# Queries and keys in fp16 parts scaled by a power of two per batch, eight head pairs in plain float32, in an attention and MLP kernel

## The chip, the core and the metric

The kernel runs on one core of a Trainium2 chip. The metric is the device time of one execution in microseconds (us). The engines are TensorE (PE, matmuls; its weight loads are listed as PEld), VectorE (DVE), ScalarE (ACT), GpSimd (POOL) and SyncE (SP), whose queue issues the DMA transfers here, in order.

## The reference

A batch of 8 with 8 heads of 64 dimensions has 512 local and 32 global tokens. Global queries attend to all 544 keys, local queries to the 32 global keys and to local keys at most 32 positions away. The output rows then go through a two-layer MLP with Mish. Cut to what matters:

```python
k_all = np.concatenate([k_g, k_l], axis=2); v_all = np.concatenate([v_g, v_l], axis=2)
s_g = scale * np.matmul(q_g, k_all.transpose(0, 1, 3, 2))      # 32 x 544 per head
out_g = np.matmul(sm(s_g), v_all)
s_ll = np.where(mask, scale * np.matmul(q_l, k_l.transpose(0, 1, 3, 2)), -1e9)   # |i - j| <= 32
s_lg = scale * np.matmul(q_l, k_g.transpose(0, 1, 3, 2))
out_l = np.matmul(sm(np.concatenate([s_lg, s_ll], axis=-1)), v_all)
x = np.concatenate([out_g, out_l], axis=2)      # to 4352 rows of 512
h = x @ w_in                                    # 512 -> 2048
return (h * np.tanh(np.log1p(np.exp(h)))) @ w_out
```

## The kernel before, in words

Attention runs over 8 batches `b` of 4 head pairs `hp`, and each pair has 4 query tiles `t` of 128 rows. One (b, hp, t) is a unit; there are 128. For a unit, both heads' scores `s` (L608, in PSUM tiles of the ring `sc`) are formed on PE against a window of 192 (t = 0 and 3) or 224 (t = 1 and 2) keys. DVE adds the mask and takes the row maximum into `P` (L614), ACT takes the exponential (L623), ACT and DVE split the result into an fp16 part `ph` and a rest (L307, L642), a DMA transposes it into `pt`, and PE multiplies it with the values into `U` (L659). Once per pair the global queries' scores `g` (L697) are formed, normalised, transposed (`gpt`) and multiplied with the values (`gu`, L745). The normalised rows are split again and transposed by DMA into `xh` and `xl`.

The MLP runs over 17 blocks of 256 rows (two per batch, and one for the global rows), each in 8 steps. A step is 24 matmuls into `h` (L788: three products of the fp16 parts of weights and rows), Mish on ACT (`e`, L831), a split into fp16 parts `G` on DVE (L309, L844), and 12 matmuls into `o` (L856). One MLP step goes with one attention unit while there are any; the last steps stand alone at the end.

Float32 operands are multiplied as parts. Of a split pair, the keys come into `kraw` and the queries into `qraw`, each head's 64 dimensions twice, on 128 partitions. `ks` is a copy of the keys rounded to the type fp32r (L541, a cast at L300 on ACT or L302 on DVE), `kl` the rest (L546). `qs` holds the rounded query on the first 64 partitions and its rest on the others (L531, L538). A score is then two matmuls of 128 rows, `ks` with `qs` and `kl` with `qs`. `g_scores` takes four products for each stretch of keys, with `qgh`, the split global queries (L503). The first NPS = 5 pairs (all four of batch 0, and one of batch 1) are "plain": their queries and keys come once, in float32, and each head's score is one float32 matmul of 64 rows (L601).

At the start, the MLP weights come as 64-bit words and are put together into float32 in 32 blocks: DVE makes two of the three pieces (L384, L393), ACT converts the third into a buffer `wr` (L386), and GpSimd adds (L395). PE sums squares of the weights (L405) for a power-of-two scale, and then the weights are split into fp16 parts (L439 to L445). The first matrix must be ready before the first `h`, the second before the first `o`.

The order of all instructions on all engines, SP's queue too, is made ahead by a planner (class `Plan`). Each task is added with its engine or engines, an estimate of its time, and what it reads, writes and newly takes from a ring of buffers; a simulation then lets each engine start the task that can begin earliest, and of several the one that was added first. A few constants (`LATE_K`, `LATE_L`, `CONV2` and the like) shift groups of tasks. Tasks whose inputs and buffers are ready early are so drawn forward into idle time of the estimate. On the chip each engine then works strictly in that order.

## Time and profile before

| | |
|---|---|
| median of 3 runs | 1020.02 us (1020.01 to 1021.5) |
| profiled execution | 1018.93 us |
| its span, first to last instruction | 1017.1 us |
| PE busy | 925.7 us, 91% |
| DVE busy | 668.5 us, 66% |
| ACT busy | 680.9 us, 67% |
| GpSimd busy | 82.2 us, 8% |
| moved by DMA | 134.65 MB, mean 132 GB/s |
| mean granted clock of PE | 0.973 |

The profile is of one execution. A group's line gives line of code, engine, operation, output and inputs with shapes and count, then busy time in us and the mean ns of one, then the idle time of the engine before them and what ended it. Matmuls overlap one another, since a matmul's time includes that in which its last columns drain; the pace is read from their starts. A timeline row gives start and length in us, and merges several of a kind (x3).

### The profile page before, as it was taken

The numbers are of one execution on the slowest core, as the hardware profiler recorded it, in microseconds if no ns is written. First come the engines' busy times: TensorE is split into PE (matmuls) and PEld (weight loads), VectorE is DVE, ScalarE is ACT, GpSimd is POOL, SyncE is SP. The second block draws the span as 40 slices with busy tenths as digits, with TensorE's granted clock in tenths as the row PEclk, the third lists the DMA queues.
The fourth block names the chain that finished last, engine by engine and source line by source line (L and its number), as shares of the span: only waits on it lengthen the run. The fifth ranks groups of instructions, "written<-read, shape, count | busy, mean of one in ns | idle before, by whom it ended". The sixth has DMA issues, their size and how long they took to land.

```text
span 1017.1 us, 20581 instructions
## 1 busy us (share of the span) xinstructions
PE 925.7 (91%) x7906; PEld 664.6 (65%) x7906; DVE 668.5 (66%) x1704; ACT 680.9 (67%) x1321; POOL 82.2 (8%) x62
## 2 busy tenths in 40 slices
PE   3455696899999999999999999999999999999996
PEld 2233475566776777677777777777777777666663
DVE  6977796887766767776677666767676655322221
ACT  3465566777897788878878888788878888211110
POOL 3725231410000000000000000000000000000000
PEclk9997588999999999999999999999999999999999
DMA  9847982587758664766557665666676544100000
GB/s 333 228 111 175 262 259 63 112 180 189 168 104 180 144 143 113 177 148 143 123 153 161 134 133 129 155 135 141 117 165 127 123 81 77 42 1 22 1 22 21
DMA packets 231802, 134.65 MB, mean 132 GB/s; under 512 B 197528, under 2 KB 209048, under 8 KB 230680
## 3 DMA queue, kind: packets, MB, share of 16 engines
q1 hardware_dynamic: 231704, 133.34, 57.1%
q8 instruction: 62, 1.02, 0.4%
q14 instruction: 36, 0.29, 0.1%
HBM read 63.55 MB, written 8.91 MB: 71 GB/s over the span
## 4 chain that ended last, share of the span: by engine, by line
PE 65%; DVE 12%; DMA 8%; ACT 4%; issue 3%; SPq 1%; POOL 0%; ACTq 0%; DVEq 0%
PE o L856 28%; PE h L788 26%; PE s L608 4%; PE U L659 3%; DMA vraw<-in_vm 3%; DMA pt<-ph 2%; PE g L697 2%; DMA gpt<-gph 2%; PE gu L745 1%; DVE vmx L481 1%; DVE P L614 1%; DVE ph L642 1%; DVE G L309 1%; SPq L296 1%; DVE kl L546 1%
## 5 line engine op out<-in xcount | busy, mean ns | idle before, releaser
L856 PE MATMUL o<-W,G 128*128 128x512 f16 x1632 | 389.8, 379 | 0.3 <-POOL W L445 0.3
L788 PE MATMUL h<-xh,W 128*128 128x256 f16 x2048 | 379.0, 275 | 5.1 <-ACT e L831 5.1
L788 PEld LDWEIGHTS <-W 128*128 128x128 f16 x3264 | 311.2, 98 | 68.6 <-issue 5.3
L788 PE MATMUL h<-xl,W 128*128 128x256 f16 x1024 | 281.0, 274 | 0.0
L856 PEld LDWEIGHTS <-G 128*128 128x128 f16 x1632 | 156.9, 98 | 144.1 <-issue 0.6
L831 ACT ACTIVATE e<-h,c 128x512 f32<-128x512 f32 (+1 forms) x137 | 92.6, 683 | 117.5 <-PE h L788 116.6
L623 ACT ACTIVATE P<-P,nm 128x192 f32<-128x192 f32 (+1 forms) x256 | 117.8, 460 | 41.5 <-DVE nm L614 40.3
L309 DVE TENSOR_SCALAR G<-e,c 128x512 f16<-128x512 f32 x129 | 63.9, 495 | 118.5 <-ACT e L831 118.4
L614 DVE CUSTOM_DVE_ANT_0 P<-s,consts 128x192 f32<-128x192 f32 (+1 forms) x256 | 90.1, 367 | 68.1 <-PE s L608 57.7
L642 DVE SCALAR_TENSOR_TENSOR ph<-P,ph 128x384 f16<-128x384 f32 (+1 forms) x128 | 78.0, 611 | 80.1 <-ACT ph L307 79.3
L844 DVE SCALAR_TENSOR_TENSOR G<-e,c,G 128x512 f16<-128x512 f32 (+1 forms) x137 | 102.0, 745 | 3.4
L831 ACT ACT_TABLE_LOAD x79 | 101.4, 1283 | 1.4
L623 ACT ACT_TABLE_LOAD x74 | 94.9, 1283 | 1.3
L659 PEld LDWEIGHTS <-pt 96*128 96x128 f16 (+1 forms) x1536 | 59.3, 101 | 33.5 <-DMA pt<-ph 26.9
L307 ACT ACTIVATE ph<-P 128x384 f16<-128x384 f32 (+1 forms) x128 | 69.7, 548 | 16.3 <-DMA pt<-ph 13.2
L659 PE MATMUL U<-va,pt 128*128 128x64 f16 (+1 forms) x768 | 59.4, 199 | 19.7 <-DMA pt<-ph 19.7
L608 PE MATMUL s<-ks,qs 128*128 128x192 f32 (+1 forms) x216 | 71.4, 353 | 1.4 <-DVE qs L538 0.9
L659 PE MATMUL U<-vc,pt 96*128 96x64 f16 x768 | 58.7, 198 | 0.0
L718 ACT ACTIVATE gP<-g,gmx 64x288 f32<-64x288 f32 x64 | 30.4, 476 | 37.5 <-DVE gmx L713 37.4
L395 POOL TENSOR_TENSOR W<-W,wr 128x512 int32<-128x512 int32 x32 | 48.8, 1535 | 79.0 <-DVE W L393 40.1
L608 PE MATMUL s<-kl,qs 128*128 128x192 f32 (+1 forms) x216 | 54.2, 274 | 0.0
L405 PE MATMUL ws<-W 128*128 128x128 bf16 x128 | 17.7, 286 | 37.4 <-POOL W L395 37.3
(103 smaller groups left out, 1024.3 us busy)
## 6 DMA issues: line engine op xcount, KB each, us to landing
kraw<-in_kt SPq DMA_DIRECT2D x27, 640.0 KB, 4.7
qraw<-in_qt SPq DMA_DIRECT2D x27, 512.0 KB, 3.8
W<-in_w SPq DMA_DIRECT2D x19, 512.0 KB, 7.1
out<-ob SPq DMA_DIRECT2D x34, 256.0 KB, 2.6
vraw<-in_vm SPq DMA_DIRECT2D x8, 1024.0 KB, 6.0
wraw<-in_w SPq DMA_DIRECT2D x13, 512.0 KB, 5.9
vc<-vf SPq DMA_DIRECT2D x32, 128.0 KB, 2.3
va<-vf SPq DMA_DIRECT2D x32, 96.0 KB, 2.3
```

Source lines behind the costliest of these rows:

```text
L307: A.activation(out=dst, in_=src, func=AF.Copy, scale=c)
L309: V.tensor_scalar(dst, src, c, None, ALU.mult)
L395: pl.add(POOL, pool(512), lambda: G.tensor_tensor(f(), f(), X["wr", k], ALU.add), r=[("wr", k)], w=[key])
L608: T.matmul(X[s][:, :w], X[qs][:, h, t * 128:(t + 1) * 128], X[k][:, h, c0:c0 + w], start=(i == 0), stop=(i == 1))
L614: pl.add(DVE, 69 + 1.04 * w, lambda: V.tensor_tensor_reduce(out=X[P][:, h, :w], in0=X[s][:, :w], in1=mask[:, m0:m0 + w], scale=-SCALE, sca ...
L623: pl.add(ACT, 160 + 0.832 * w + 93, lambda: A.activation(out=X[P][:, h, :w], in_=X[P][:, h, :w], func=AF.Exp, bias=X[nm], scale=-1.0, accu ...
L642: pl.add(DVE, dve(n), lambda: V.scalar_tensor_tensor(p_part(X[ph], t, 1), p_src(X[P], t), PSC, p_part(X[ph], t, 0), ALU.mult, ALU.subtract ...
L659: T.matmul(X[u][:, t, h, :], X[pt][:k, p * 4 + h * 2 + c, :], X[vx][:k, t, vl, h * 64:(h + 1) * 64], start=(n == 0), stop=(n == 5))
L788: T.matmul(X[h][:, f * TB:(f + 1) * TB], wh(i, wl)[:, off:off + 128], X[x][:, d, o:o + TB], start=(n == 0), stop=(n == 11))
L831: chain(blk, i, ACT, 571, lambda a, z: A.activation(out=X[e][:, a:z], in_=hv(blk, i)[:, a:z], func=AF.Mish, bias=0.0, scale=X[c][:, 0:1]), ...
L844: chain(blk, i, DVE, 602, lambda a, z: V.scalar_tensor_tensor(gp(1, blk, i)[:, a:z], X[e][:, a:z], X["c", blk][:, 2:3], gp(0, blk, i)[:, a ...
L856: T.matmul(X[o], gp(g, blk, i)[:, f, t * 128:(t + 1) * 128], wh(8 + i, wl)[:, f * 512:(f + 1) * 512], start=(i == 0 and n == 0), stop=(i = ...
```

## The change

Queries and keys of the split pairs are now split into fp16 parts in place of fp32r. Since fp16 has a small range, keys are first multiplied by a power of two, and queries by its inverse, so that products stay as they are; one power per batch, chosen so that the largest query and the largest key of the batch get about the same size. It comes from a new input `mxs`, which holds all queries and keys of a batch once more in four tiles of 128 x 1088. `b_norm` loads these tiles, takes the largest absolute value of each on DVE, joins them across partitions on GpSimd and makes the two factors `sk` in some ten instructions on one column. It runs for batches 2 to 7. The first eight pairs, batches 0 and 1, are plain float32, in tiles `kn` and `qn` of their own, and need no factors; the four tiles of `mxs` go through the same buffers `kn` (`kraw` for batch 2). To make room, the ring `wr` goes from two buffers to one.

The estimate of the two score matmuls goes from `mm(2, 262)` to `mm(2, 235)`; all other estimates of steps that remain, and all constants, stand as they were.

```diff
-NPS = 5
+NPS = 8
...
-          ("wr", 2, [128, 512], I32),
+          ("wr", 1, [128, 512], I32),
...
-          ("qs", 2, [128, 2, SL], F32R), ("ks", 2, [128, 2, KW], F32R), ("kl", 2, [128, 2, KW], F32R),
-          ("qgh", 2, [128, 3, HP, 64], F32R), ("vgf", 2, [128, 2, 128], F16),
+          ("qs", 2, [128, 2, SL], F16), ("ks", 2, [128, 2, KW], F16), ("kl", 2, [128, 2, KW], F16), ("qgh", 2, [128, 2, HP, 64], F16),
+
+          ("qn", 2, [128, 2, SL], F32), ("kn", 2, [128, 2, KW], F32), ("mx4", 1, [128, 4], F32), ("m4", 1, [128, 4], F32),
+          ("sk", 2, [128, 4], F32), ("vgf", 2, [128, 2, 128], F16),
...
+    def b_norm(b):
+        mx, m, sk = ("mx4", b), ("m4", b), ("sk", b)
+        for i in range(4):
+            k = ("kn", "m", b, i)
+            ring = "kraw" if b == 2 else "kn"
+            pl.add(DMA, dma(544), lambda i=i, k=k: load(X[k].rearrange("p a n -> p (a n)")[:, :1088], mxs[b, i]), new=[(ring, k)])
+            pl.add(DVE, dve(1088), lambda i=i, k=k: V.tensor_reduce(
+                out=X[mx][:, i:i + 1], in_=X[k].rearrange("p a n -> p (a n)")[:, :1088], axis=AX.X, op=ALU.max,
+                apply_absolute_value=True), r=[k], w=[[mx, i]] if i else (), new=() if i else [("mx4", mx)])
...
     def q_hi(b, hp):
-        pl.add(COPY(1024, b), 0, lambda e: copy(e, X[qs], X[q]), r=[q], new=[("qs", qs)])
+        pl.add(COPY(1024, b), 0, lambda e: scaled(e, X[qs], X[q], X["sk", b][:, 0:1]), r=[q, ("sk", b)], new=[("qs", qs)])
...
     def k_lo(b, hp, h):
-        pl.add(DVE, dve(640), lambda: V.tensor_tensor(X[kl][:, h], X[k][:, h], X[ks][:, h].bitcast(F32), ALU.subtract),
-               r=[k, ks], w=[[kl, h]], new=() if h else [("kl", kl)])
+        pl.add(DVE, dve(640), lambda: V.scalar_tensor_tensor(X[kl][:, h], X[k][:, h], X["sk", b][:, 1:2], X[ks][:, h], ALU.mult, ALU.subtract),
+               r=[k, ks, ("sk", b)], w=[[kl, h]], new=() if h else [("kl", kl)])
...
-        pl.add(PE, mm(2, 262), go, r=[qs, ks, [kl, h]], new=[("sc", s)])
+        pl.add(PE, mm(2, 235), go, r=[qs, ks, [kl, h]], new=[("sc", s)])
...
-        if u == 11:
-            for n in range(HP, NPS):
-                plain_load(1, n - HP, "ks", kt0, KW)
-                plain_load(1, n - HP, "qs", qt0, SL)
+        if u in (8, 15):
+            for n in ((4, 5), (6, 7))[u == 15]:
+                plain_load(1, n - HP, "kn", kt0, KW)
+                plain_load(1, n - HP, "qn", qt0, SL)
...
+            if hp == (b > 1) and t == 2:
+                b_norm(b + 1)
```

`q_lo`, `k_hi` and `g_split` change in the same way, and `g_scores` uses the two fp16 parts that `qgh` now holds.

Three places show what moves. First PE, in batch 4, pair 2, tile 1: `gu` are the global values of the pair before, `s` the scores by batch, pair, tile and head. Before:

```order
L745 LDWEIGHTS vf_4_1_5765
L745 MATMUL gu_4_1_6435<-gpt_4_1_6400,vf_4_1_5765 128x64
L608 MATMUL s_4_2_1_0_6453<-ks_4_2_5949,qs_4_2_5895 128x224
L608 MATMUL s_4_2_1_0_6453<-kl_4_2_5960,qs_4_2_5895 128x224
L608 MATMUL s_4_2_1_1_6456<-ks_4_2_5949,qs_4_2_5895 128x224
L608 MATMUL s_4_2_1_1_6456<-kl_4_2_5960,qs_4_2_5895 128x224
L659 LDWEIGHTS pt_4_1_3_6339
```

In the changed kernel:

```order
L780 MATMUL gu_4_1_6532<-gpt_4_1_6486,vf_4_1_5816 128x64
L643 LDWEIGHTS qs_4_2_5946
L643 MATMUL s_4_2_1_0_6548<-ks_4_2_6000,qs_4_2_5946 128x224
L643 LDWEIGHTS qs_4_2_5946
L643 MATMUL s_4_2_1_0_6548<-kl_4_2_6011,qs_4_2_5946 128x224
L643 LDWEIGHTS qs_4_2_5946
L643 MATMUL s_4_2_1_1_6553<-ks_4_2_6000,qs_4_2_5946 128x224
```

The fp32r matmuls carry their weight load with them; the fp16 ones have a weight load as an instruction of its own ahead of each, like all other fp16 matmuls here.

Second, SP's queue in the start-up, just after the transposes `xh`, `xl` of batch 0's last pair, which the first `h` needs. `W` and `wraw` are weight blocks, `kn_m_2` the new tiles for batch 2. Before:

```order
L467 DMA_TRANSPOSE xl_0_638<-xs_0_3_1125 128x4x128
L296 DMA wraw_28_1167<-in_w2 128x1024
L296 DMA W_70<-in_w2 128x1024
L296 DMA qraw_1_1_1194<-in_qt 128x1024
L467 DMA_TRANSPOSE pt_1_0_1_1217<-ph1_73 128x8x128
L296 DMA kraw_1_2_1239<-in_kt 128x1280
L296 DMA wraw_30_1264<-in_w2 128x1024
L296 DMA W_70<-in_w2 128x1024
```

In the changed kernel:

```order
L469 DMA_TRANSPOSE xl_0_618<-xs_0_3_1113 128x4x128
L298 DMA W_70<-in_w2 128x1024 x2
L469 DMA_TRANSPOSE pt_1_0_1_1175<-ph1_73 128x8x128
L298 DMA kn_m_2_0_1200<-in_mxs 128x1088
L298 DMA W_70<-in_w2 128x1024
L298 DMA wraw_28_1232<-in_w2 128x1024
L298 DMA qraw_2_0_1263<-in_qt 128x1024
L298 DMA kn_m_2_1_1271<-in_mxs 128x1088
L469 DMA_TRANSPOSE gpt_1_0_1310<-gph0_80 128x10x64
L298 DMA W_70<-in_w2 128x1024
L298 DMA kn_m_2_2_1360<-in_mxs 128x1088
L298 DMA wraw_30_1395<-in_w2 128x1024
```

The loads of batch 1's split pairs are gone from this place; the tiles of `mxs` stand there in turn with the last weight blocks, three more of which now come after these transposes than before.

Third, DVE in batch 2, pair 1. `c` are the MLP's factors, `vf` the split values, `P` the row maximum of scores. Before:

```order
L770 TENSOR_TENSOR c_4_3023<-sv_2_2366,iw_67 128x1
L772 TENSOR_SCALAR c_4_3023<-sv_2_2366,sw_68 128x1
L642 SCALAR_TENSOR_TENSOR ph0_72<-P_2_1_0_2976,ph0_72 128x4x96
L561 SCALAR_TENSOR_TENSOR vf_2_2_3066<-vraw_2_2173,sv_2_2366,vf_2_2_3066 128x4x128
L614 ISA P_2_1_1_3089,nm_2_1_1_0_3090<-s_2_1_1_0_3070,consts_65 128x224
```

In the changed kernel:

```order
L805 TENSOR_TENSOR c_4_3110<-sv_2_2398,iw_67 128x1
L514 TENSOR_REDUCE mx4_4_3114<-kn_m_4_0_2956 128x1
L807 TENSOR_SCALAR c_4_3110<-sv_2_2398,sw_68 128x1
L514 TENSOR_REDUCE mx4_4_3114<-kn_m_4_1_2999 128x1
L649 ISA P_2_1_1_3160,nm_2_1_1_0_3161<-s_2_1_1_0_3138,consts_65 128x224
L649 ISA nm_2_1_1_0_3161 128x1
L596 SCALAR_TENSOR_TENSOR vf_2_2_3158<-vraw_2_2260,sv_2_2398,vf_2_2_3158 128x4x128
```

Reduces for batch 4 stand inside batch 2, two batches ahead of their use, between steps that feed the units. Of the 24 reduces, five stand before the first row maximum of batch 2, 14 between it and that of batch 3 (the rest of batch 3's, all of batches 4 and 5, and three of batch 6), and five after.

More of the change, by code (lines that the diff above doesn't have):

```diff
@@ new lines, in g_split @@
+    def g_split(b):
+        q, rq, sk = ("qgh", b), ("qgraw", b), ("sk", b)
+        pl.add([(ACT, act(512)), (DVE, dve2(512))], 0, lambda e: scaled(e, X[q], X[rq][:, 1:3], X[sk][:, 0:1]), r=[rq, sk], new=[("qgh", q)])
+        for a, h in ((0, HI), (1, LO)):
+            pl.add(DVE, dve(256), lambda a=a, h=h: V.scalar_tensor_tensor(X[q][h, a], X[rq][h, 1 + a], X[sk][h, 0:1], X[q][h, a], ALU.mult,
+                                                                          ALU.subtract), r=[rq, sk], w=[[q, a]])
@@ L994, in slot @@
             b_scale(b + 1)
-            g_split(b + 1)
             b_split(b + 1)
```

61 lines of the change are left out of this document (40 added, 21 removed).

## The prediction

> **What bounds the kernel now.** I read the sums of the engines first, then the busy times by stage, then the timeline of TensorE to get the pace of each kind of matmul.
>
> ```profile
> PE 925.7 (91%) x7906; PEld 664.6 (65%) x7906; DVE 668.5 (66%) x1704; ACT 680.9 (67%) x1321; POOL 82.2 (8%) x62
> ```
>
> The windows, in the columns PE, PEld, DVE, ACT, POOL, granted clock, DMA share and GB/s, say where that share is limiting.
>
> ```profile
> 120.00:132.00 12.00, 7.44 (x50) 4.98 (x47) 10.82 (x22) 6.56 (x17) 5.87 (x4) 0.50 1.03 266
> ...
> 140.00:160.00 20.00, 16.10 (x154) 14.14 (x152) 18.73 (x35) 11.38 (x21) 5.12 (x3) 1.00 0.57 172
> 160.00:180.00 20.00, 14.61 (x124) 10.87 (x123) 11.97 (x31) 14.41 (x20) 3.48 (x4) 0.83 0.36 75
> 180.00:200.00 20.00, 17.31 (x153) 11.30 (x152) 17.85 (x31) 13.83 (x30) 10.81 (x5) 1.00 0.46 83
> 200.00:220.00 20.00, 17.77 (x146) 11.03 (x145) 15.91 (x44) 15.43 (x35) 4.38 (x3) 1.00 0.89 189
> 220.00:320.00 100.00, 97.93 (x917) 72.16 (x916) 73.35 (x201) 77.75 (x153) 0.91 (x2) 1.00 0.71 154
> 320.00:840.00 520.00, 516.23 (x4685) 381.21 (x4683) 367.02 (x1002) 426.65 (x809) 1.40 (x4) 1.00 0.64 139
> ...
> 880.00:1017.00 137.00, 127.16 (x868) 84.74 (x866) 31.35 (x56) 21.57 (x32) 0.00 (x0) 0.98 0.05 16
> ```
>
> From 220 us on PE idles 2.1 us of 100 and then 3.8 us of 520, at full clock. What shortens PE's own work there comes off the end, so long as the others keep up; DVE is at 73% and 71%, ACT at 78% and 82%. From 140 to 220 us PE lacks 3.9, 5.4, 2.7 and 2.2 us (14.2 in all), with DVE as busy as 18.73 of 20: that is the end of the start-up, where other engines set the pace. The last stretch is MLP alone, which the change leaves.
>
> **The pace of the matmuls.** A matmul's own duration includes its drain, so I take starts. Two long runs from the chain of waits give the fp16 pace:
>
> ```profile
> 880.84 2.62 PE h L788 x24
> ...
> 1000.69 6.49 PE o L856 x30
> ```
>
> That is 109 ns for 256 columns and 216 ns for 512: 0.418 ns per column, hence 82 ns at 192 columns and 96 ns at 224. Now a fp32r score group (four matmuls: two heads, ks and kl), after `gu` and after `o`, on the timeline:
>
> ```profile
> 538.37 0.35 PE L608 MATMUL s<-ks,qs 128*128 128x224 f32 x1
> 538.56 0.27 PE L608 MATMUL s<-kl,qs 128*128 128x224 f32 x1
> ...
> 538.90 1.47 PE L856 MATMUL o<-W,G 128*128 128x512 f16 x6
> 540.01 0.45 PE L608 MATMUL s<-ks,qs 128*128 128x224 f32 x1
> ...
> 540.64 0.28 PE L788 MATMUL h<-xh,W 128*128 128x256 f16 x1
> ```
>
> After `gu` the group holds PE 538.90 - 538.37 = 0.53 us. After `o`, its first matmul begins while `o` drains, so I count both: 540.64 - 538.90 = 1.74 us, less six `o` at 0.216, leaves 0.44 us. The global scores `g`, with three fp16 U matmuls as a yardstick in the first two rows:
>
> ```profile
> 521.91 0.25 PE L659 MATMUL U<-va,pt 128*128 128x64 f16 x3
> 522.00 0.25 PE L659 MATMUL U<-vc,pt 96*128 96x64 f16 x3
> 522.09 0.43 PE L697 MATMUL g<-ks,qgh 128*64 128x256 f32 x2
> ...
> 522.59 0.24 PE L697 MATMUL g<-ks,qgh 128*64 128x32 f32 x2
> ...
> 522.79 0.42 PE L697 MATMUL g<-ks,qgh 128*64 128x256 f32 x2
> ...
> 523.30 0.28 PE L788 MATMUL h<-xh,W 128*128 128x256 f16 x1
> ```
>
> Twelve `g` matmuls take 1.21 us, the four short ones among them 0.20, 50 ns each, while three fp16 ones of 64 columns take 0.09 us, 30 ns each, although each brings its own 128-column weights. The weight loads differ, too:
>
> ```profile
> L608 PEld LDWEIGHTS s<-kl,qs 128*128 128x128 f32 x216 | 41.3, 191 | 2.2
> ...
> L659 PEld LDWEIGHTS <-pt 96*128 96x128 f16 (+1 forms) x1536 | 59.3, 101 | 33.5 <-DMA pt<-ph 26.9 <-issue 2.7
> ```
>
> So the fp32r group is held at about 110 ns per matmul whatever its width, and fp16 loads of 101 ns overlap down to 30 ns. The Trainium skill, "TensorE: Matmul & The Clock Gate", section "Weight-path perf modes — Fast Weight Load (FWL) and DoubleRow", puts the fast load on for 128 weight columns of any type but FP32; the 191 and 101 ns agree with that.
>
> **The change, part by part.**
>
> *Scores of the 24 pairs that stay split.* In fp16 a group costs 4 x 96 = 0.383 us at t = 1 and 2, 4 x 82 = 0.33 at t = 0 and 3. In each pair one group (t = 1) follows `gu`: 24 x (0.53 - 0.383) = 3.5 us. The other 72 average 0.347: 72 x (0.44 - 0.347) = 6.7 us. Sum -10.2 us.
>
> *Global scores.* Eight of 0.109 and four at the 30 ns pace are 0.99 us, so 24 x (1.21 - 0.99) = -5.3 us. The weights here have 64 columns, not 128; if the four short ones kept their 50 ns, 24 x 0.08 us of it would be lost, so the bounds are -3.4 and -5.3.
>
> *Three more pairs in plain float32.* The trace has these at the low clock:
>
> ```profile
> 126.93 3.96 PE L601 MATMUL s<-ks,qs 64*128 64x224 f32 x12
> 130.82 1.27 PE L697 MATMUL g<-ks,qgraw 128*64 128x256 f32 x4
> ```
>
> Twelve start within 3.89 us at clock 0.50 (window 120:132): 0.65 us a group of two, 0.33 at full clock, against 0.44 to 0.53. Twelve groups save 12 x 0.13 = 1.5 us; the `g` of these pairs I count even. They lie in 140 to 220 us, where PE has gaps: between 0 and -1.5, I take -1.5.
>
> *DVE.* Removed with three pairs, and added with each reduce and each scale:
>
> ```profile
> L844 DVE SCALAR_TENSOR_TENSOR G<-e,c,G 128x512 f16<-128x512 f32 (+1 forms) x137 | 102.0, 745 | 3.4
> ...
> L642 DVE SCALAR_TENSOR_TENSOR ph<-P,ph 128x384 f16<-128x384 f32 (+1 forms) x128 | 78.0, 611 | 80.1 <-ACT ph L307 79.3
> ...
> L546 DVE TENSOR_TENSOR kl<-kraw,ks 128x640 fp32r<-128x640 f32 x54 | 44.3, 821 | 0.2 <-ACT ks L300 0.2
> ...
> L538 DVE TENSOR_TENSOR qs<-qraw,qs 64x1024 fp32r<-64x1024 f32 x27 | 33.0, 1223 | 0.8
> ...
> L481 DVE TENSOR_REDUCE vmx<-vraw 128x1 f32<-128x512 f32 x32 | 20.6, 678 | 11.6 <-DMA vraw<-in_vm 11.6
> ...
> L485 DVE TENSOR_REDUCE vmx<-vgraw 128x1 f32<-128x128 f32 x8 | 2.2, 271 | 0.0
> ...
> L500 DVE TENSOR_TENSOR pmax<-pmax,p 128x1 f32<-128x1 f32 x8 | 1.2, 150 | 0.0
> ```
>
> Gone: 3 x (2 x 0.821 + 1.223) = 8.6 us besides the copies. The copies that remain become scaled copies of the same width, on the same two engines; I cost that at nothing. The subtraction becomes a three-operand instruction: the first two rows give (745 - 611)/128 = 1.05 ns a column, so 0.88 us for 640 columns instead of 0.82; about 0.06 us on each of three instructions in 24 pairs is 4 us over the whole run. New: a reduce over 1088 columns is 0.678 + 576 x 1.06 = 1.29 us ((678 - 271)/384 = 1.06 ns a column); four, and some ten small instructions of 0.15 us, for each of six batches: 40 us. The MLP and attention on PE hide them as long as DVE is not full. The order says where they stand: 5 of the 24 reduces before batch 2, 14 with three scale chains inside batch 2, 5 after. In batch 2 (220 to 320 us) DVE goes from 73.35 to 73.35 + 14 x 1.29 + 3 x 1.5 = 96 us, in a stage that PE, with 16 score groups and 4 global ones shortened, would finish in 97.4. Two stretches bound what that costs:
>
> ```profile
> 220.00:240.00 20.00, 20.00 (x196) 15.08 (x195) 18.48 (x61) 14.17 (x35) 0.56 (x1) 1.00 0.80 172
> ```
>
> Here DVE is at 92% and PE loses nothing; at 140:160 DVE is at 94% and PE loses 3.9 of 20, which over 100 us is 19. I take +3, near the first, which is the steady order; bounds 0 and 19. What waits behind a late reduce on DVE is the row maximum of the next scores, which frees the score banks that PE's next scores need.
>
> *Loads.* Each of the 24 new loads stands on SP's queue ahead of transposes and weight loads. With 43% of DMA time free at 160:220 on average and 36% at 320:840, I cost the steady ones at nothing; that cover is gone where DMA runs at 1.03, as at 120:132.
>
> *One `wr` buffer.* ScalarE may convert the next weight block only after GpSimd has added the last:
>
> ```profile
> 22.42 11.93 POOL L395 TENSOR_TENSOR W<-W,wr 128x512 int32<-128x512 int32 x8 [8.21 <-DVE W L393]
> 36.07 1.31 POOL L395 TENSOR_TENSOR W<-W,wr 128x512 int32<-128x512 int32 x1 [1.72 <-DVE W L393]
> 38.08 1.31 POOL L395 TENSOR_TENSOR W<-W,wr 128x512 int32<-128x512 int32 x1 [0.69 <-DVE W L393]
> ...
> L386 ACT ACTIVATE wr<-W x19: 654/679/701, 26.8 to 143.6; 128x512 int32<-128x512 uint32 x19
> ```
>
> Eight adds back to back take 1.49 us each, the next ones come every 2.01 us. An add of 1.31 and a conversion of 0.68 in turn, with two handovers, make about 2.2: 8 x 0.7 + 8 x 0.2 = 7 us later for the first matrix. It is needed only by the first `h`, which the last transposes of batch 0 hold until 132 us, so I take 0; bounds 0 and +7. Against it, the freed splitting can close up to about 9 of the 14.2 us that PE lacks there: -9.
>
> *Sum*, against the profiled execution (1018.93 us, its span 1017.1): -10.2 - 5.3 - 1.5 + 3 = -14.0, so 1004.9. The median of the three runs before, 1020.02, is 1.1 above the profiled one: forecast 1006.
>
> **The rivals.**
>
> *A: DVE overflows in batch 2, and the kernel is slower.* The new reduces are in order on DVE, so each also waits when its load is late. The nearest row:
>
> ```profile
> DVE vmx L481 <- DMA vraw<-in_vm: 11.6, 6, 3.3
> ```
>
> It shows 1.9 us a wait (the third number is the longest). With 14 x 1.9 = 27 us of waits beside 96 of work, DVE needs 25 us more than the 97.4 there are, and the kernel takes 1006 - 3 + 25 = 1028. It ends slower than before when a reduce waits over (17 + 1.4)/14 = 1.3 us on average. For it: the loads of several batches are drawn into batch 2. Against: only 6 of 32 reduces of `vmx` waited so, and a planned order that runs late on PE gives loads more time. Chance 0.16.
>
> *B: the start-up shortens as well.* 8.6 us and copies leave DVE where it is 94% busy; with 9 of the 14.2 us back the time is 997. Against: batch 2's first two pairs and five reduces move forward into the same place. Chance 0.16.
>
> *C: the start-up lengthens.* The single buffer's 7 us reach the first `h`, since DVE, ACT and SP work strictly in order: 1013. Chance 0.13.
>
> *D: fp16 weight loads do not overlap here*, so that the change does not do for the scores what it says. At the 101 ns of the load's row a group is 0.404 us and saves 72 x 0.036 + 24 x 0.126 = 5.6 instead of 10.2: 1011. Against: the U matmuls at 30 ns. Chance 0.05. The Trainium skill, "TensorE: Matmul & The Clock Gate", section "LDWEIGHTS (loading the stationary operand)", prices a load at its columns over 1.2 per ns, which is 107 ns for 128: by that rule as the pace the saving would be 3.3 us; the measured 30 ns pace speaks against reading it so.
>
> **How the numbers follow.** The forecast has 0.50, A 0.16, B 0.16, C 0.13, D 0.05. The forecast's own bounds are about 1000 to 1013. The range 995 to 1021 takes in B, C and D and the beginnings of A; what it leaves out is most of A (0.13) and the tail of B (0.04). A measurement of this kernel can tell about 0.2%, 2 us, from no change. Faster: 0.48 of the forecast, all of B and D, 0.10 of C: 0.79. Same: 0.02 of the forecast, 0.02 of C and 0.02 of A: 0.06. Slower: the rest of A and a rest of C: 0.15.
>
> **What would show it.** Right: score matmuls in fp16 at 82 and 96 ns from start to start, a `g` group near 1.0 us, PE still without gaps from about 220 us, DVE near 96 of 100 in batch 2, and the first `h` at 132 us, give or take 5. Wrong: a pace of 101 ns (D); gaps of PE in front of `s` in batch 2, ended by DVE, with reduces that wait for their loads (A); a first `h` several us later, behind ACT conversions that wait for GpSimd (C), or no gaps left before 220 us (B).

## The result, and the profile after

| | before | changed |
|---|---|---|
| median, same chip | 1020.76 us (1020.01 to 1023.34, 4 runs) | 1032.82 us (1030.22 to 1035.34, 4 runs) |
| ratio, 95% interval | | 1.0115 (1.0088 to 1.0142) |
| profiled execution, span | 1018.93, 1017.1 us | 1033.34, 1031.5 us |
| mean granted clock of PE | 0.973 | 0.952 |

Slower by 12 us, where the forecast was 14 less and its range ended at 1021. The sums of the engines on the page of the changed kernel:

```profile
PE 924.3 (90%) x7888; PEld 640.8 (62%) x7888; DVE 691.8 (67%) x1763; ACT 668.6 (65%) x1314; POOL 86.1 (8%) x68
```

A matmul's busy time includes its drain, so this sum hides what became of PE; the pace shows it. First a score group, second a group of `g` between two `h`, on the timeline of the changed kernel:

```profile
562.87 0.25 PE L643 MATMUL s<-ks,qs 128*128 128x192 f16 x1
...
563.20 0.25 PE L694 MATMUL U<-va,pt 128*128 128x64 f16 x3
...
564.76 0.27 PE L823 MATMUL h<-xh,W 128*128 128x256 f16 x1
564.96 0.41 PE L732 MATMUL g<-ks,qgh 128*64 128x256 f16 x2
...
565.42 0.21 PE L732 MATMUL g<-ks,qgh 128*64 128x32 f16 x2
565.48 0.21 PE L732 MATMUL g<-kl,qgh 128*64 128x32 f16 x2
...
565.77 0.38 PE L732 MATMUL g<-kl,qgh 128*64 128x256 f16 x2
566.08 0.28 PE L823 MATMUL h<-xh,W 128*128 128x256 f16 x1
```

The score group takes 563.20 - 562.87 = 0.33 us, as forecast. The `g` group takes 566.08 - (564.76 + 0.109) = 1.21 us, what it took in fp32r. Its short matmuls did come down to the 30 ns of `U` (0.06 us a pair); what was won is lost at its two ends: 564.96 is 0.09 us after the last `h` has gone through, and 566.08 comes 0.09 us after the last `g` (565.77 + 2 x 0.109).

The plain scores at full clock, in batch 1, on the timeline, and their row among the groups of the whole run:

```profile
220.60 0.65 PE L636 MATMUL s<-kn,qn 64*128 64x224 f32 x4
221.18 0.26 PE L694 MATMUL U<-va,pt 128*128 128x64 f16 x3
...
221.64 0.74 PE L636 MATMUL s<-kn,qn 64*128 64x224 f32 x4
222.31 0.39 PE L891 MATMUL o<-W,G 128*128 128x512 f16 x1
```

```profile
L636 PE MATMUL s<-kn,qn 64*128 64x192 f32 (+1 forms) x128 | 41.1, 540 | 12.8 <-DVE nm L649 8.3 <-DMA qn<-in_qt 4.4
```

Eight pairs of four tiles and two heads are 64 matmuls in the program; the trace lists 128. A float32 matmul leaves two records, so a group of four records is one tile: 0.58 and 0.67 us, more than the 0.44 to 0.53 of fp32r.

The windows that answer to those of before (PE, PEld, DVE, ACT, POOL, granted clock, DMA share, GB/s):

```profile
140.00:160.00 20.00, 17.40 (x147) 14.31 (x146) 19.37 (x28) 11.14 (x18) 8.96 (x6) 0.88 0.75 253
160.00:180.00 20.00, 14.23 (x134) 12.50 (x132) 13.28 (x37) 8.63 (x14) 4.07 (x5) 0.89 0.22 68
180.00:200.00 20.00, 16.97 (x136) 10.46 (x134) 16.78 (x30) 19.07 (x24) 6.91 (x4) 0.77 0.58 153
200.00:220.00 20.00, 18.22 (x126) 9.20 (x121) 13.93 (x31) 12.65 (x30) 10.97 (x5) 1.00 0.90 166
220.00:320.00 100.00, 93.00 (x827) 60.98 (x828) 76.79 (x214) 66.04 (x147) 2.18 (x3) 1.00 0.80 186
320.00:840.00 520.00, 510.00 (x4715) 364.34 (x4716) 391.08 (x1050) 420.00 (x808) 4.16 (x8) 1.00 0.69 151
```

PE now lacks 7.0 us at 220:320 (2.1 before) and 10.0 at 320:840 (3.8 before). From 140 to 220 it lacks 13.2, about as before, and the clock is down for longer: 0.88, 0.89 and 0.77 take 2.4 + 2.2 + 4.6 = 9.2 us of clock away (part of it while PE waits anyway), against 3.4 in the one window at 0.83. DVE, which I had at 96 of 100 at 220:320, is at 76.79. What PE waits for longest from 300 to 880 us, first in the changed kernel, then before (us in all, times, longest):

```profile
PE gu L780 <- DMA gpt<-gph: 6.2, 8, 1.4
PE U L694 <- DMA pt<-ph: 4.1, 6, 1.5
```

```profile
PE U L659 <- DMA pt<-ph: 3.9, 5, 1.8
PE gu L745 <- DMA gpt<-gph: 1.3, 4, 0.4
```

These are waits for transposed tiles: 10.3 us in place of 5.2.

The account below is made in the same way for every run of this case. For each profiled execution it has the start of the first `h`; PE's idle time from there to its last matmul; what half clock cost in between, which is half of PE's busy time in the stretches whose granted clock is 0.50; and the rest, PE's work from the first `h` on at full clock. The last matmul ends 10.0 to 10.5 us ahead of the end of the span in every kernel, and with these 10 us the four add up to the span.

| kernel | median us | ratio to before | span | first h | PE idle | half clock | PE work |
|---|---|---|---|---|---|---|---|
| before | 1020.8 | 1 | 1017.1 | 132.0 | 20.1 | 4.4 | 850.7 |
| changed | 1032.8 | 1.0115 | 1031.5 | 138.0 | 30.2 | 7.8 | 845.3 |
| after_wr2 | 1027.3 | 1.0053 | 1020.8 | 132.9 | 27.8 | 3.4 | 846.7 |
| before_wr1 | 1032.4 | 1.0112 | 1033.3 | 147.3 | 20.8 | 5.5 | 849.8 |
| after_no_norm | 1027.2 | 1.0054 | 1023.7 | 138.4 | 25.2 | 5.1 | 845.0 |
| after_no_norm_wr2 | 1019.2 | 0.9980 | 1020.5 | 134.6 | 23.7 | 6.9 | 845.1 |
| before_nps8 | 1030.9 | 1.0094 | 1028.2 | 133.1 | 23.3 | 6.0 | 855.8 |
| fp16_only | 1020.7 | 0.9996 | 1020.5 | 132.0 | 28.0 | 11.3 | 839.2 |
| after_g128 | 1032.6 | 1.0120 | 1033.8 | 138.9 | 34.5 | 11.4 | 839.0 |
| after_held | 1020.7 | 1.0002 | 1020.7 | 139.0 | 20.0 | 8.0 | 843.6 |
| after_wr2_held | 1012.4 | 0.9929 | 1007.8 | 133.5 | 16.3 | 2.7 | 845.2 |
| after_wr2_held_g128 | 1009.1 | 0.9891 | 1006.6 | 134.2 | 20.0 | 3.3 | 839.0 |
| fp16_only_late | 1010.8 | 0.9903 | 1009.0 | 144.7 | 14.4 | 4.3 | 835.2 |
| before_late | 1017.5 | 0.9969 | 1016.2 | 144.2 | 11.0 | 2.6 | 848.3 |
| after_late | 1030.3 | 1.0085 | 1028.3 | 147.9 | 17.0 | 10.1 | 843.4 |
| after_wr2_held_g128_late | 1034.8 | 1.0135 | 1036.3 | 139.8 | 37.9 | 10.7 | 838.0 |
| after_late_b3 | 1025.2 | 1.0044 | 1022.7 | 137.6 | 23.8 | 8.3 | 843.0 |
| after_wr2_held_g128_late_b3 | 1014.8 | 0.9946 | 1016.8 | 133.9 | 24.8 | 8.2 | 839.9 |

For the changed kernel: first `h` +6.0, idle +10.1, half clock +3.4, work -5.4, in all 14.1 of the 14.4 us between the two spans. Kernels that do the same matmuls agree within 4 us in the last column (843.0 to 846.7 for those with the changed kernel's matmuls); work before the first `h` is not in it, and the planner can move work across that point. A profiled span can also stand some us off its median: single runs of one kernel spread over 2 to 8 us.

### The profile page after: what moved, and what is told of

Its sections match the earlier page's. It is cut to its first block, busy times and chain, and to the rows that moved or that the text cites. A ratio compares the mean times of both kernels' runs of the same rounds, so it can differ in the third digit from the quotient of the medians.

```text
span 1031.5 us, 20592 instructions
## 1 busy us (share of the span) xinstructions
PE 924.3 (90%) x7888; PEld 640.8 (62%) x7888; DVE 691.8 (67%) x1763; ACT 668.6 (65%) x1314; POOL 86.1 (8%) x68
## 4 chain that ended last, share of the span: by engine, by line
PE 56%; DVE 14%; DMA 12%; ACT 5%; issue 3%; SPq 1%; POOL 0%; DVEq 0%; ACTq 0%
PE h L823 24%; PE o L891 23%; DMA gpt<-gph 5%; DMA pt<-ph 4%; PE U L694 2%; PE s L643 2%; PE g L732 2%; DMA vraw<-in_vm 2%; DMA kn_m<-in_mxs 1%; DVE ph L677 1%; DVE G L879 1%; PE gu L780 1%; DVE P L649 1%; DVE kl L581 1%; DVE mx L514 1%
## 5 line engine op out<-in xcount | busy, mean ns | idle before, releaser
L311 DVE TENSOR_SCALAR G<-e,c 128x512 f16<-128x512 f32 (+1 forms) x128 | 62.9, 492 | 117.9 <-ACT e L866 117.6
L694 PEld LDWEIGHTS <-pt 96*128 96x128 f16 (+1 forms) x1536 | 64.3, 102 | 40.9 <-DMA pt<-ph 30.0
L309 ACT ACTIVATE ph<-P 128x384 f16<-128x384 f32 (+1 forms) x128 | 69.5, 546 | 16.8 <-DMA pt<-ph 14.1
L397 POOL TENSOR_TENSOR W<-W,wr 128x512 int32<-128x512 int32 x32 | 46.6, 1457 | 78.3 <-ACT wr L388 28.6
L636 PE MATMUL s<-kn,qn 64*128 64x192 f32 (+1 forms) x128 | 41.1, 540 | 12.8 <-DVE nm L649 8.3
L658 ACT ACTIVATION_READ_ACCUMULATOR P<-P,nm 128x1 f32 x256 | 47.8, 187 | 0.0
```

Source lines behind the costliest of these rows:

```text
L309: A.activation(out=dst, in_=src, func=AF.Copy, scale=c)
L311: V.tensor_scalar(dst, src, c, None, ALU.mult)
L397: pl.add(POOL, pool(512), lambda: G.tensor_tensor(f(), f(), X["wr", k], ALU.add), r=[("wr", k)], w=[key])
L636: pl.add(PE, mm(1, 4 * w), lambda: T.matmul(X[s][:, :w], X[q][r, part, t * 128:(t + 1) * 128], X[k][r, part, c0:c0 + w], start=True, stop= ...
L658: pl.add(ACT, 160 + 0.832 * w + 93, lambda: A.activation(out=X[P][:, h, :w], in_=X[P][:, h, :w], func=AF.Exp, bias=X[nm], scale=-1.0, accu ...
L694: T.matmul(X[u][:, t, h, :], X[pt][:k, p * 4 + h * 2 + c, :], X[vx][:k, t, vl, h * 64:(h + 1) * 64], start=(n == 0), stop=(n == 5))
```

## The experiments

### The single buffer: after_wr2 and before_wr1

```
-          ("wr", 1, [128, 512], I32),
+          ("wr", 2, [128, 512], I32),
```

in the changed kernel; the reverse in the kernel before.

> The changed kernel with two wr buffers in place of one, and nothing else. Theory 1 (the single buffer delays the first weight matrix by 9 us, and that delay of the start-up stays to the end): GpSimd's adds come at 1.5 to 2.0 us again in place of 2.1, the sums of squares of the first matrix end near 52 us in place of 61.5, the first h falls back from 138 to about 132 us, and the median goes from 1032.8 to about 1022 to 1026. Rival (the loads and reduces of the largest values cause the loss, the buffer only fills time that was free): under 3 us, so 1030 to 1033.

> The kernel before with one wr buffer in place of two, and nothing else. Theory 1: the first matrix is ready about 9 us later, the first h comes 4 to 9 us later than 132 us, and the median is 1025 to 1030 against 1020.8. Rival (the buffer costs nothing, since the first h is held by batch 0's last transposes at 132 us): 1019 to 1023.

Measured: after_wr2 1027.29 us, 1.0053 (1.0038 to 1.0068); before_wr1 1032.38 us, 1.0112 (1.0091 to 1.0132). The first gains 5.5 us, a little less than the theory had, the second loses 11.5, more than it had. With one buffer the adds of the changed kernel come at a fixed pace (timeline of GpSimd):

```profile
37.63 1.33 POOL L397 TENSOR_TENSOR W<-W,wr 128x512 int32<-128x512 int32 x1 [0.79 <-ACT wr L388]
39.76 1.33 POOL L397 TENSOR_TENSOR W<-W,wr 128x512 int32<-128x512 int32 x1 [0.80 <-ACT wr L388]
```

That is 2.13 us an add, the 2.2 of the prediction. What it does to PE is seen in the longest wait of before_wr1 between 100 and 150 us:

```profile
PE ws L405 <- POOL W L395: 16.6, 7, 4.8
```

The sums of squares wait 16.6 us (4.7 before), and the first `h` starts at 147.3, 15 us late. In the changed kernel the same buffer costs 5.1 us of first `h`. So the 7 us of delay do reach the first `h`; that batch 0's transposes would cover them is refuted, and the size depends on the order around them: 5 in one, 15 in the other.

### The search for the factors: after_no_norm and after_no_norm_wr2

`b_norm` is cut down to one memset; the factors are 1, and loads and reduces of `mxs` and the search for the power of two are left out.

```
-        for i in range(4):
...
+        pl.add(DVE, 70, lambda: V.memset(X[sk][:, 0:2], 1.0), new=[("sk", sk)])
```

> The changed kernel without the search for the largest query and key: both factors are set to 1, so the 24 loads of 557 KB, the 24 reduces and the small instructions behind them are left out; one wr buffer stays. Rival theory (these loads and reduces are the loss): most of the 12 us comes back and more, 1010 to 1020. Theory 1 (the buffer is the main loss): the first h stays near 138 us, only what batches 1 and 2 lose on PE and DVE comes back, some 5 to 7 us, so 1025 to 1028.

> The changed kernel without the search for the largest values (factors 1; loads, reduces and small instructions are left out) and with two wr buffers: what stays are fp16 parts and eight plain pairs. If the three costs simply add, 1032.8 - 5.5 - 5.6, so 1021 to 1023; if the three added plain pairs cost the 10 us that they cost alone, and fp16 saves 10, also about 1021. If the buffer and the loads delay the same wait, one hides the other: 1025 to 1028.

Measured: after_no_norm 1027.2 us, 1.0054 (1.0037 to 1.0072); after_no_norm_wr2 1019.21 us, 0.998 (0.9968 to 0.9992). The first is within the range of the theory that the buffer is the main loss; the second is under both of its ranges. Without any of the new loads and reduces, and with both buffers, the kernel is only 0.2% faster than before, although its work on PE is that of the changed kernel (845.1 us). Loads, reduces and buffer are thus not the whole gap to the forecast: PE idles 23.7 us after the first `h`, and half clock costs 6.9.

### Parts of the change alone: before_nps8 and fp16_only

before_nps8 is the kernel before with eight plain pairs, their loads and `qgraw` placed as in the changed kernel. fp16_only is the kernel before with fp16 parts: five plain pairs (in the tiles `kn` and `qn` of the changed kernel), two buffers, factors of 1 and no search for them.

```
-NPS = 8
+NPS = 5
...
-          ("wr", 1, [128, 512], I32),
+          ("wr", 2, [128, 512], I32),
```

(the two main lines in which fp16_only differs from after_no_norm; the loads of the plain pairs and of `qgraw`, and the splitting of `qgraw`, go back to their places in the kernel before.)

> The kernel before with eight plain pairs in place of five, loaded and placed as in the changed kernel; the other pairs stay in fp32r, without factors, with two wr buffers. If the three pairs only shorten DVE's work at the end of the start-up, as the prediction has it: 1012 to 1019. If the earlier loads of the plain pairs, ahead of the last weight blocks on SP, are what delays the second matrix by 11 us: 1024 to 1031.

> The kernel before with one part of the change alone: split queries and keys in fp16 parts. Five plain pairs, two wr buffers, no search for the largest values (both factors are 1, set once per batch; the loads and reduces of mxs are left out). The score groups were measured at 0.33 and 0.385 us in fp16 against 0.44 and 0.53. If that is worth what the prediction's term says, 27 pairs save about 11 us, and with the start-up untouched the median is 1008 to 1013. If faster scores only turn into waits of PE, since the planned order of the other engines holds it, 1016 to 1022.

Measured: before_nps8 1030.85 us, 1.0094 (1.0068 to 1.0119); fp16_only 1020.66 us (10 runs), 0.9996 (0.998 to 1.0011). The plain pairs add 5.1 us of work, in place of taking 1.5 away, and 4.8 us of idle and half clock beside it. The first `o` starts at 174.8, before at 176.2: the time came out where the theory of a delayed second matrix had it, but not by that delay. Whether the earlier loads or the longer matmuls make the waits was not separated. In fp16_only work falls by 11.5 us, just what the prediction's 10.2 for 24 pairs makes for 27, and the time does not move: idle is up 7.9 (2.5 of it from 300 to 880 us) and half clock 6.9. The waits of PE from 300 to 880 us have one row:

```profile
PE U L670 <- DMA pt<-ph: 7.7, 5, 2.2
```

The longest of the five, on the timeline:

```profile
526.05 0.26 PE L670 MATMUL U<-va,pt 128*128 128x64 f16 x3 [2.17 <-DMA pt<-ph]
```

and in the windows around that place:

```profile
523.78:527.19 3.41, 1.24 (x22) 1.09 (x22) 3.16 (x9) 2.97 (x7) 0.00 (x0) 1.00 0.92 125
527.19:530.60 3.41, 3.41 (x19) 2.24 (x17) 3.31 (x7) 0.59 (x2) 0.00 (x0) 0.50 0.17 38
```

PE stands 2.17 us before `U`, for a transpose; DVE and ACT are busy meanwhile (3.16 and 2.97 of 3.41). Then the clock is at half for 3.41 us, which costs another 1.7 us. From 300 to 880 us it falls so at 319, 527 and 735. A wait of 2.21 us in before_nps8, from 487.86 to 490.07, left the clock at full:

```profile
485.13:488.55 3.42, 2.73 (x34) 2.33 (x33) 1.93 (x5) 2.13 (x5) 0.00 (x0) 1.00 1.17 125
488.55:491.96 3.41, 1.89 (x23) 1.27 (x23) 0.12 (x1) 1.22 (x3) 0.00 (x0) 1.00 1.05 215
```

The traces tell the two apart. In each of the 18 profiled executions all falls of the clock after 150 us lie on one grid of 3.41 us, the windows shown here, which stands at another place in each execution. Of the windows of these grids at full clock, up to 985 us, all 42 in which PE was busy for less than 1.45 us were followed by half clock; of those between 1.45 and 1.85 us seven of 16 were, and of 4210 above that none. The wait of 2.17 us fell into one window, and the one of 2.21 us into two.

### The weight columns of g: after_g128

`qgh` has a spare head of zeros at its end, so that each `g` matmul can load 128 columns, this head's and the next one's; the 64 further output rows are not read.

```
-          ("qgh", 2, [128, 2, HP, 64], F16)
+          ("qgh", 2, [128, 2, HP + 1, 64], F16)
...
-products([(X[q][:, h, hp, :], X[k][:, h])
+products([(X[q][:, h, hp:hp + 2, :].rearrange("p a c -> p (a c)"), X[k][:, h])
```

> The changed kernel, but each global score matmul loads 128 weight columns (its own pair's 64 and the next pair's, or zeros, whose 64 output rows nobody reads) in place of 64. In the changed kernel a group of twelve global score matmuls took 1.21 us, as in fp32r, with gaps of 0.1 us before and behind it. If the 64-column load is what holds the group, it takes about 1.0 us, 24 x 0.2 less on PE, and the median is 1026 to 1031. If fp16 products of 256 columns are simply no faster here, it stays 1.21 us and the median stays 1030 to 1035.

Measured: 1032.62 us, 1.012 (1.0099 to 1.0141), the time of the changed kernel (1032.82) and not the 1026 to 1031 expected. The group itself became what the prediction had it at:

```profile
568.53 0.27 PE L824 MATMUL h<-xh,W 128*128 128x256 f16 x1
568.64 0.38 PE L733 MATMUL g<-ks,qgh 128*128 128x256 f16 x2
...
569.40 0.38 PE L733 MATMUL g<-kl,qgh 128*128 128x256 f16 x2
569.61 0.27 PE L824 MATMUL h<-xh,W 128*128 128x256 f16 x1
```

569.61 - 568.64 = 0.97 us, without a gap at either end. So it is the 64 weight columns that cost 0.24 us a group. Their loads, first in the changed kernel, then here:

```profile
L732 PEld LDWEIGHTS <-qgh 128*64 128x64 f16 x288 | 22.2, 111 | 5.0 <-issue 4.7 <-ACT ph L309 0.2
L733 PEld LDWEIGHTS <-qgh 128*128 128x128 f16 x288 | 21.0, 97 | 2.7 <-issue 0.5
```

A load of 64 columns takes 111 ns, one of 128 columns 97. The Trainium skill, "TensorE: Matmul & The Clock Gate", section "Weight-path perf modes — Fast Weight Load (FWL) and DoubleRow", which I cited for the type, makes 128 weights the other condition of the fast load. These 111 and 97 ns agree with that; the loss itself stands mostly at the group's two ends (0.18 of the 0.24 us). In the account work falls by 6.3 us, and idle and half clock rise by 7.9. The longest waits from 300 to 880 us:

```profile
PE gu L781 <- DMA gpt<-gph: 7.4, 8, 2.5
PE U L695 <- DMA pt<-ph: 6.6, 6, 3.0
```

14.0 us in place of 10.3: a second saving on PE that went into waits, most of them for transposes, and into half clock.

### The place of the new loads: after_wr2_held, after_held, after_wr2_held_g128

Each load of `mxs` must come, in the planner's eyes, after the row maximum of the third tile of the pair in which it is added, one batch ahead of its use. It is the same work; the planner can no longer draw it further forward.

```
-    def b_norm(b):
+    def b_norm(b, hp):
+        held = pl.state[pl._key(("nm", b - 1, hp, 2, 0))[0]][None][0]
...
+            pl.tasks[-1][2].add(held)
```

> The changed kernel with two wr buffers, and with each batch's loads of mxs held by the planner until the row maximum of tile 2 of the batch before (a planned order alone, nothing waits for it on the chip), so that they are not drawn two batches forward. If crowding in batches 1 to 3 is what the loads and reduces cost, about 4 us come back against the run with two buffers alone (1027.3): 1022 to 1025. If they cost the same wherever they stand, 1026 to 1029.

> The changed kernel with its single wr buffer, and the loads of mxs held in the order until the row maximum of the third tile, second or third pair, of the batch before. Theory (two separate costs: the early loads and reduces of mxs cost PE waits between the first h and batch 3 and clock after them, the single wr buffer costs some 5 us ahead of the first h): with only the first cost cured the time is that of the kernel with two buffers and held loads, 1012.4, plus 5 to 6: 1017 to 1018; first h at 138 as in the changed kernel, PE idle from the first o to 300 us near 3.5 in place of 9.1. Rival (the gain of the held loads depends on the second buffer, because the last weight blocks of the second matrix are what they collided with): 1025 to 1030, with PE idle to 300 us still at 7 or more.

> The changed kernel with two wr buffers, held loads and 128 weight columns in the g matmuls (the 64 further output rows are not read). Theory (PE's saving reaches the time only where the other engines' results are there): with few waits left in this order (4.3 us from 300 to 880), most of 24 x 0.24 = 5.7 us of g arrives, 1007 to 1009. Rival (every further saving on PE turns into waits of the same length, as it did with g128 on the changed kernel): 1012 to 1013, with PE idle from 300 to 880 up from 4.3 to 9 or 10.

Measured: after_wr2_held (two buffers) 1012.38 us, 0.9929 (0.9906 to 0.9951); after_held (one buffer) 1020.71 us, 1.0002 (0.9988 to 1.0017); after_wr2_held_g128 (also 128 columns in `g`) 1009.11 us, 0.9891 (0.9874 to 0.9909), the fastest here. after_wr2_held is 10 us faster than the better of its two expectations. What held loads mean in batch 2 shows in PE's waits for transposes from 220 to 320 us, first in the changed kernel, then in after_wr2_held:

```profile
PE U L694 <- DMA pt<-ph: 5.3, 5, 1.9
PE gu L780 <- DMA gpt<-gph: 2.0, 2, 1.3
```

```profile
PE gu L782 <- DMA gpt<-gph: 0.3, 1, 0.3
```

and in the transfers of the same 100 us (KB of one, median us from issue to landing), the changed kernel first:

```profile
kn_m<-in_mxs SPq DMA_DIRECT2D x10, 544.0 KB, 5.2
...
pt<-ph SPq DMA_TRANSPOSE x16, 3.8
```

```profile
kn_m<-in_mxs SPq DMA_DIRECT2D x4, 544.0 KB, 4.0
...
pt<-ph SPq DMA_TRANSPOSE x18, 3.1
```

Ten tiles of `mxs` went through SP's queue in these 100 us, among the transposes, which landed after 3.8 us in place of 3.1; with four tiles PE's waits for transposes fall from 7.3 to 0.3. That the tiles themselves hold up the transposes is true of a part only. The first of the ten is issued at 260.84, and 4.0 of the 7.3 us lie ahead of it. The longest of those stands behind a load that the kernel before has, too (SP's issues, then PE):

```profile
232.09 2.04 SPq L298 DMA_DIRECT2D vraw<-in_vm  x1
234.25 1.28 SPq L469 DMA_TRANSPOSE pt<-ph  x1
240.71 0.26 PE L694 MATMUL U<-va,pt 128*128 128x64 f16 x3 [1.88 <-DMA pt<-ph]
```

Only two waits, 1.3 us at 220.06 and 1.9 us at 268.31, are for a transpose issued within 2.1 us behind a tile of `mxs`. And in the kernel before, with no such tile, the transposes of these 100 us land after 3.5 us and PE waits 2.0 us. The rest came with the other order. DVE does about the same work in both (76.79 and 78.58 of 100). Holding the loads is worth 12 us with one buffer, more than the 5.6 that leaving them out altogether is worth (after_no_norm): the order that comes with a load weighs more than the load. after_held came out between what the two theories expected: the 10 us of idle are gone, but the later first `h` (139.0) and half clock from 155 to 195 us stayed as they were. Of the 24 x 0.24 = 5.8 us that 128 columns save, about 3 arrived; PE idle from 300 to 880 rose from 4.3 to 8.0, so each theory has a part of it.

### A later landing in the planner: fp16_only_late and before_late

The planner is told that transposes land 1.0 us later than it assumed. No instruction is added; the matmuls that read transposed tiles are placed later on PE.

```
-                done[n] = t + self.DMA_IN + ns + self.DMA_OUT
+                done[n] = t + self.DMA_IN + ns + self.DMA_OUT + self.lands.get(n, 0)
```

with `lands` 1000 ns for each `turn`.

> The kernel before with the fp16 parts alone (five plain pairs, two wr buffers, factors set to 1), and the planner told that each DMA transpose lands 1.0 us later than it assumed, so that the matmuls that read transposed tiles stand later on PE. No instruction is added or removed. Theory (the 11.4 us that fp16 takes off PE's work were lost in waits of U and gu for transposed tiles, which the order places too early once PE is faster, and in half-clock stretches after them): waits of U for pt from 300 to 880 go from 7.7 us to under 2, no half-clock stretch there, and the time from 1020.7 to 1008 to 1013. Rival (the order is only a symptom; ACT, DVE or the queue of transfers is what bounds each unit, and matmuls placed later wait for something else): within 3 us of 1020.7, with the same PE idle put down to other tiles, or to the steps behind the later units.

> Control: the kernel before, with the same 1.0 us later landing of transposes in the planner. Theory: its steady stage lost only 5.7 us of PE idle and no clock from 300 to 880, so no more than 4 us are to be had, and the start-up may shift by as much either way: 1015 to 1024. Rival (a later landing time is simply the better planner constant, whatever the type of the scores): 1008 to 1013, the same 8 to 12 us gain as with fp16 parts.

Measured: fp16_only_late 1010.81 us, 0.9903 (0.9881 to 0.9924); before_late 1017.53 us, 0.9969 (0.9953 to 0.9985). All that PE still waits for transposes from 300 to 880 us in fp16_only_late:

```profile
PE gu L758 <- DMA gpt<-gph: 0.4, 1, 0.4
```

0.4 us where `U` alone had 7.7, no half clock there, and 10 us less, although its first `h` comes 13 us later. The kernel before gains 3.6 from the same edit (idle from 300 to 880 from 5.7 to 0.2). So most of the fp16 saving was there all the time, and was lost in an order that no longer fitted PE's pace: with the later landing in both, fp16 parts are worth 1017.53 - 1010.81 = 6.7 us of the 11.5 that they take off PE's work.

### The same in the changed kernel: after_late and after_wr2_held_g128_late

> The changed kernel, and the planner told that each DMA transpose lands 1.0 us later; the mxs loads, the reduces and the single wr buffer stay. Theory (most of the PE idle after 300 us is matmuls placed too early for their transposed tiles): idle from 300 to 880 us from 11.9 to under 3, the start-up as late as before or some us later, and the time 1019 to 1024. Rival (the mxs loads and their reduces are what delays the transposes in the steady stage, by their place in the queue and on DVE): idle from 300 to 880 stays over 7, and the time over 1027.

> The changed kernel with all four edits: two wr buffers, held mxs loads, 128 weight columns in g, and the later landing time. Theory (the three causes are the whole gap): idle from 300 to 880 under 2 in place of 8.0, and 1000 to 1005, the forecast or a little under it, since g is repaired too. Rival (the later landing time only moves waits into the start-up, whose first h it delayed by 12 us in the kernel before with fp16 parts): 1008 to 1013, no better than without it.

Measured: after_late 1030.29 us, 1.0085 (1.0056 to 1.0114); after_wr2_held_g128_late 1034.81 us, 1.0135 (1.0107 to 1.0164). Both are slower than their theories had them. In after_late the steady waits did go: of the 10.3 us for transposes between 300 and 880,

```profile
PE U L696 <- DMA pt<-ph: 1.7, 4, 0.8
```

is left of it, and idle there fell from 11.9 to 4.8, with as many `mxs` loads and reduces as before. The rival that these alone delay the transposes falls with that; that their place has a part shows in after_held, where the same idle is 7.2. But its first `h` starts at 147.9, 10 us late, and eats most of it. In the other kernel the start-up broke, as its two longest waits from 100 to 300 us show:

```profile
PE o L896 <- DVE W L312: 10.1, 1, 10.1
PE o L896 <- POOL W L448: 9.8, 1, 9.8
```

The planner put the first `o` at a place where the second matrix was not yet split; PE waits for it twice, is busy 2.58 of 20 us at 160:180, and works on at half clock.

### Only from batch 3 on: after_late_b3 and after_wr2_held_g128_late_b3

```
+        if r[0][1] > 2:
+            pl.lands[len(pl.tasks) - 1] = 1000
```

> The changed kernel, with the landing 1.0 us later for transposes of batch 3 and later alone; the order of PE is unchanged up to some 300 us. Theory (two separate causes): first h at 138, third o block at 285 as in the changed kernel, PE idle from 300 to 880 us from 11.9 to under 5, and 1023 to 1027, 6 to 10 under the changed kernel. Rival (a later place for U only moves the same wait to other tiles): idle over 8 and 1030 to 1034.

> Two wr buffers, held mxs loads, 128 weight columns in g, and the landing 1.0 us later for transposes of batch 3 and later alone. Theory: start-up as in the same kernel without it (first h 134, third o block 270), idle from 300 to 880 from 8.0 to under 3, and 1002 to 1006. Rival: idle over 6 and 1008 to 1011.

Measured: after_late_b3 1025.21 us (10 runs), 1.0044 (1.0031 to 1.0057); after_wr2_held_g128_late_b3 1014.84 us, 0.9946 (0.9926 to 0.9966). The first kept its start-up (first `h` 137.6) and lost 7 us of idle after 300 us (11.9 to 5.0): 7.6 us less time from the planner's estimate alone, as the theory had it. The second went the other way, 5.7 us up on the same kernel without the edit and slower than both expectations. Its longest waits from 260 to 880 us, in a profiled execution 3.8 us above the median:

```profile
PE U L700 <- DMA pt<-ph: 3.8, 4, 1.3
PE h L829 <- ACT e L872: 3.4, 4, 1.3
PE gu L786 <- DMA gpt<-gph: 3.1, 2, 2.7
```

Half clock came back three times (328, 434 and 642 us). Why the new order makes `gu` wait 2.7 us once and `h` 3.4 us in four places for ACT is not shown. A later landing is thus no better constant in general: each edit yields another order, good or bad, and only its account tells which.

## Why the prediction was wrong

**What PE loses by, in steady state: the step that failed.** The prediction read "what shortens PE's own work there comes off the end, so long as the others keep up", and took busy shares of 73% and 82% as proof that they would. fp16_only refutes it: 11.5 us of work gone, no time won. PE hardly waited because the order fitted its pace, with transposes landing just in time; with faster scores and the same assumed landing it reached `U` ahead of them. The free share of DVE and ACT did not tell how long the chain score, maximum, exponential, split, transpose, `U` takes.

**Scores.** Right: 0.33 us a group at 192 columns (rival D is out), and work falls with it as forecast (fp16_only). For this term the forecast failed in what becomes of the work, not in its size.

**Global scores.** -5.3 came out at 0, outside my bounds. I had seen that the weights have 64 columns, and priced only the short matmuls with it; the loss is mostly at the group's ends, and 128 columns remove it (0.97 us).

**Plain pairs.** -1.5 became +5.1 (work of before_nps8). I counted x12 records of L601 as twelve matmuls; they are six, three tiles in 3.89 us at half clock, 0.65 us a tile at full clock against some 0.46 in fp32r. For 12 tiles that is 2.3 us; where the rest of the 5.1 comes from is open. With the scores' -10.2 and nothing from `g`, the three terms make -5.1, and the account has -5.4.

**DVE, and rival A.** The reduce was sized right:

```profile
L514 DVE TENSOR_REDUCE mx<-kn_m 128x1 f32<-128x1088 f32 x24 | 30.6, 1274 | 6.0 <-DMA kn_m<-in_mxs 6.0
```

1.27 us against 1.29. But DVE is at 76.79 from 220 to 320 us, not 96. Nine of the 14 reduces fell into this stretch (11.4 us), and only four `kl` and two `qs` are split in it, where it was eight and five before (6.1 us in place of 12.6): I added all reduces to a stage and took nothing out of it. Rival A named the right stage and a nearly right time (1028), by a wrong cause: all 24 reduces wait 6.0 us together, 0.25 each in place of 1.9, and PE waits in front of `U` for transposes, not in front of `s` for DVE.

**Loads.** "I cost the steady ones at nothing" failed: with the loads held, 7.0 of the 7.3 us of waits from 220 to 320 us are gone, and the whole kernel gains 12. About 3.2 us of them were for transposes right behind a tile of `mxs`; the rest came with the order. The free share of DMA time, 43% and 36%, was no cover for a transpose that stands behind a large load.

**One `wr` buffer.** Taken at 0, with 7 as a bound: the first `h` came 6.0 us late, 5.1 of them by the buffer (after_wr2). That is rival C. The 9 us that freed splitting was to give back in the start-up (rival B) did not come.

**Half clock** had no term. It cost 3.4 us more than before, all of it before 200 us.

Sum by these steps: forecast -14.0, measured +14.4 (spans), a difference of 28.4, of which the steps make 28.1: PE's work 11.6 (it fell 5.4, not 17.0), idle 7.1 (+10.1, not +3), first `h` 6.0, half clock 3.4. What stays open is how far the parts depend on each other: against before, alone, they cost +11.5 (before_wr1), +9.9 (before_nps8) and -0.7 (fp16_only), and together with the search for the factors +12. They do not add up, since each makes another order.

## What to carry to other kernels

In a kernel whose order is planned from estimates, price an edit in two parts: the work of the bounding engine, which can be worked out from paces, and the fit of the order, which can't; unless the estimates follow the new pace, take a saving on PE as lost in waits until the trace shows otherwise. When such an edit disappoints, split the span into first use, idle, half clock and work before blaming an instruction; here that showed less work of PE in every kernel with fp16 parts, and that the place of loads and the assumed landing of transposes, without one instruction less, decide as much: holding the loads back gave 12 and 15 us, and the later landing anything from 10 us less to 26 us more. Check how many records one instruction leaves before dividing a duration by a count.

## What the runs showed of the hardware that was not expected

- A group of twelve fp16 matmuls with 64 weight columns among 128-column ones takes 1.21 us, against 0.97 with 128 columns, and pays about 0.09 us at each end. The narrower load takes longer, 111 ns against 97.
- A float32 matmul is two records in the trace: 128 for 64.
- The clock falls by windows of 3.41 us, not by the length of a wait. A wait of 2.17 us within one window (PE busy for 1.24 of 3.41 us) was followed by 3.41 us at half clock, and a wait of 2.21 us across two was not; no window with PE busy for more than 1.85 us was followed by half clock, and all with less than 1.45 us were. The Trainium skill, "TensorE: Matmul & The Clock Gate", section "What's actually happening", puts the fall after an idle window of about 3.4 us. The length of the window agrees; but here it need not be idle, only busy for less than about half of it.
- A transpose that SP issued 2.2 us behind a load of 1024 KB landed after 6.4 us, where the median of its kind was 3.8.
